# Weight sums behind the gates, transposes spread over other pairs, and maxima's rows read ahead of values and keys in an mLSTM cell with a feed-forward block

## The chip, the cores and the metric

The kernel runs on one core of a Trainium2 chip. The metric is the device time of one execution in microseconds, the median of several runs. Three runs of the kernel before took 471.5, 471.28 and 469.67 us: median 471.28.

The core has five engines with queues of their own, each of which works through its instructions in the order of the program: PE (TensorE, matmuls; "PEld" is its weight load), DVE (VectorE), ACT (ScalarE), POOL (GpSimd) and SP, which here only issues DMAs. An instruction waits, with all that is behind it in its queue, until the semaphores that it names have the values it asks for.

## The reference

An mLSTM cell over 4 batches, 8 heads, 768 steps and a head size of 40, and then a feed-forward block with a quick GELU on its output (3072 tokens, 320 to 2048 to 320). All is float32.

```python
for t in range(S):
    m_new = np.maximum(f_gate[:, :, t] + m, i_gate[:, :, t])
    f_stab = np.exp(f_gate[:, :, t] + m - m_new)
    i_stab = np.exp(i_gate[:, :, t] - m_new)
    m = m_new
    C = f_stab[:, :, None, None] * C + i_stab[:, :, None, None] * np.einsum('bhd,bhe->bhde', vt, kt)
    n = f_stab[:, :, None] * n + i_stab[:, :, None] * kt
    h_tilde = np.einsum('bhde,bhe->bhd', C, qt)
    nq = np.einsum('bhd,bhd->bh', n, qt)[:, :, None]
    denom = np.maximum(np.abs(nq), 1.0)
    o = 1.0 / (1.0 + np.exp(-o_gate[:, :, t]))
    y[:, :, t] = o * h_tilde / denom
...
h = x @ w_in
g = h * (1.0 / (1.0 + np.exp(-1.702 * h)))
return (g @ w_out).astype(np.float32)
```

## The kernel before

The 768 steps are worked on in six chunks `w` = 0 to 5 of 128 steps. Within a chunk the recurrence is written as attention with weights: scores of queries and keys, times a matrix of exponentials, times values, plus a part that comes from the carried state. The main loop takes one chunk's feed-forward block at a time, and lays the attention of the next chunk beside it. It has two phases.

**Up phase** of chunk `w` (here for `w` from 1): `token_sums` (L679 to L684), and then `up_fast(w, j)` for the pairs `j` = 0 to 7, each the product of the tokens with two blocks of 128 hidden units. A Strassen-like scheme is used, so each pair has seven products of 128x256 on PE (L722) and sums around them. In one pair, ACT copies the first product `p1` out of PSUM (L761), DVE forms two sums with the second bank `p56` (L762, L763), then two more with row 1 of the result (L774, L775). ACT applies the GELU to the pair before (L690, first half 1, then half 0), copies row 0 to SBUF (L739), and POOL adds the sums to it (L781). For the last two pairs DVE does that add instead (L783). In pairs 0 and 4 the products of the last 64 input rows of four pairs are made together (L701, 16 matmuls on two halves of 64 rows). PSUM banks: p1, p56 and the rows of most pairs share four banks of the pool `ps_m`; rows of pairs 2, 3, 6 and 7 are in `ps_a`. Which bank a tile gets is settled when the program is built, and with it which reader of an older tile PE must wait for.

Beside the up phase of `w` stands the preparation of `w + 1`:
- `gates(w + 1)` after pair 0, on DVE: two running scans (L288, L296), with L290 between them (two operands in SBUF), and small steps up to `both` (L325, L326). It issues on SP the DMAs of the maxima to DRAM (`m_row`, L304 and two of L307), of the stacked gates (`st_row`, L330) and of `both` (`d_row`, L331).
- `load` brings the o gate (`eo`, 640 KB), the values (`v_st`, 640 KB in 3 DMAs) and the keys (`k_st`, 640 KB in 3 DMAs), in pieces of 160 bytes.
- `columns_in` reads `st_row` and `d_row` back as columns (`raw`, four DMAs L350 and one L352); `spread` reads `m_row` back, copied to all partitions (`wt`, four DMAs of 256 KB, L403).
- `block_transposes(w + 1, n)` for n = 0 to 7 turns the keys (even n) and queries (odd n) of one batch on DVE (L394).
- In chunk 1 only, `weight_sums(j)` for j = 0 to 3, on POOL: sums of the output weights (L803), which the down phase needs.
- `hidden_difference` (L812) and `hidden_sums` (L820, L823) prepare the down phase, mostly on POOL.

**Down phase** of chunk `w`: 14 products `down_fast` (L844 on PE, added up by DVE in L849), and after some of them a step of the attention of `w + 1`: `columns` (L367, L371 on ACT), `scale` (values times weights, `vw`, L588 on POOL), `decay` (L579), `weights` (32 exponentials on ACT, L435, and a triangular mask on POOL, L439), `carry` (L602 on PE; needs `vw` and the keys), `scores` (L459 on PE, product on DVE, L462), `values` (p_o, L503, and p_i, L511, on PE). L511's bank is that of the second half of the scores, so it comes free with the second L462.

Chunk 0 has ordinary products (L626, L635, L790) in place of the fast ones. Chunk 5 has no next chunk.

The order on each engine is the order in which the code calls; nothing reorders it. POOL's queue in chunk 1's up phase is L781 of pair 0, L803, L781 of pair 1, L803, L781 of pair 2, L803, L812, L781 of pair 3, L803, and so on. SP's queue from the last stretch of one down phase on is: keys and queries of `w + 1` in squares (8 DMAs of 320 KB, L108), the o gate, the five DMAs of the gates, values, keys, `raw`, `wt`, the gate inputs of `w + 2` (L92). SP and ACT share eight semaphores for their DMAs: each DMA waits until the one that last used its semaphore, about eight before it, has landed.

`wait_for(x)` (L590) copies one column of `x` to a tile `mark` on POOL, so that POOL's queue stands until `x` is there. The kernel before uses it once, in chunk 0.

Of the kernel before, what the change touches and what calls it, by code (L numbers as in the profile page):

```python
# [8 lines left out]
FP = mybir.dt.float32  # L9
# [17 lines left out]
def kernel(  # L27
# [14 lines left out]
    BH = B * H  # L42
# [17 lines left out]
    gate = ctx.enter_context(tc.tile_pool(name="gate", bufs=2))  # L60
# [49 lines left out]
    def load(w, what, bs=slice(0, B)):  # L110
        hs = slice(bs.start * H, bs.stop * H)
        for c in what:
            if c == "o" and w not in eo:
                eo[w] = ld.tile([L, BH, D], FP, tag="eo", bufs=1, name="eo")
            dst, src = {"k": (k_of(w), k), "q": (q_st, q), "v": (v_st, v), "o": (eo.get(w), o_gate)}[c]
            if w and c in "kv":
                for i, t, r in ((0, slice(0, L), slice(0, L)), (1, slice(0, HL), slice(HL, L)),
                                (1, slice(HL, L), slice(0, HL))):
                    x = src[:, :, w * L + t.start:w * L + t.stop, :].rearrange("b (p two) s d -> two s (b p) d", two=2)
                    nc.sync.dma_start(out=dst[r, i::2, 0:D], in_=x[i])  # L120
                continue
            nc.sync.dma_start(out=dst[:, hs, 0:D],
                              in_=src[bs, :, w * L:(w + 1) * L, :].rearrange("b h s d -> s (b h) d"))
# [98 lines left out]
    state = [const.tile([128, BH // 2, D1], FP, name=f"state{i}") for i in range(2)]  # L222
    state_mid = const.tile([128, BH // 2, D1], FP, name="state_mid")

    m_at = {0: m0}
    cols, stacked, m_row, raw = {}, {}, {}, {}
    kT, qT, ys, xT, gs, o_ps, sums, vw, x_row = {}, {}, {}, {}, {}, {}, {}, {}, {}

# [53 lines left out]
    def gates(w):  # L282
        m = m_at[w]
        swapped = gate.tile([3 * BH, L], FP, bufs=1, name="f_run")
        f_run = swapped[0:BH, :]
        m_run = gate.tile([BH, L], FP, bufs=1, name="m_run")
        st = stacked[w] = gate.tile([3 * BH, L], FP, bufs=1, name="st")
        V.tensor_tensor_scan(out=f_run, data0=ones, data1=f_sb[w], initial=0.0, op0=OP.mult, op1=OP.add)  # L288
        a = st[0:BH, :]
        V.tensor_tensor(out=a, in0=i_sb[w], in1=f_run, op=OP.subtract)  # L290
        if w == 0:
            room = work.tile([L, H, D1], FP, tag="u", name="room").rearrange("p h d -> p (h d)")
            neg, part = room[0:BH, 0:L], room.bitcast(BF)[0:BH, 2 * L:3 * L]
            V.tensor_tensor(out=neg, in0=f_run, in1=i_sb[w], op=OP.subtract)
            split(G, a3, neg, neg, part)
        V.tensor_tensor_scan(out=m_run, data0=ones, data1=a, initial=m, op0=OP.mult, op1=OP.max)  # L296
        if w == 0:

            room = work.tile([L, H, D1], FP, tag="u", name="room").rearrange("p h d -> p (h d)")
            left, part = room[0:BH, 0:L], room.bitcast(BF)[0:BH, 2 * L:3 * L]  # L300
            split(V, m3, m_run, left, part)
        else:
            to = m_row[w] = rows.tile([2, BH, HL], FP, name="m_row")
            side_queue(w).dma_start(out=to[:, 0::2].rearrange("n h t -> h n t"),  # L304
                              in_=m_run[0::2].rearrange("h (n t) -> h n t", t=HL))
            for n in range(2):
                side_queue(w).dma_start(out=to[1 - n, 1::2], in_=m_run[1::2, n * HL:(n + 1) * HL])  # L307
        end = m_run[:, L - 1:L]
        if w + 1 < NW:
            m_at[w + 1] = gate.tile([BH, 1], FP, name="m_end")  # L310
            V.tensor_tensor(out=m_at[w + 1], in0=f_run[:, L - 1:L], in1=end, op=OP.add)

        mid = m_run[:, HL - 1:HL]
        for x, (old, new) in enumerate(((m, mid), (mid, end)) if w else ((m, end),)):
            t = slice(x * HL, x * HL + HL) if w else slice(0, L)
            V.tensor_scalar(out=st[BH:2 * BH, t], in0=m_run[:, t], scalar1=old, scalar2=None, op0=OP.subtract)
            V.tensor_scalar(out=st[2 * BH:3 * BH, t], in0=a[:, t], scalar1=new, scalar2=-1.0, op0=OP.subtract,
                            op1=OP.mult)
        if w:
            for x in range(2):  # L320
                V.tensor_scalar(out=swapped[:, x * HL:(x + 1) * HL], in0=st[:, (1 - x) * HL:(2 - x) * HL], scalar1=odd,
                                scalar2=None, op0=OP.mult)
            V.scalar_tensor_tensor(out=swapped, in0=st, scalar=even, in1=swapped, op0=OP.mult, op1=OP.add)
            both = gate.tile([BH, 2], FP, name="both")
            V.tensor_tensor(out=both[:, 0:1], in0=m, in1=mid, op=OP.subtract)  # L325
            V.tensor_tensor(out=both[:, 1:2], in0=mid, in1=end, op=OP.subtract)  # L326
            st_row = rows.tile([L // 32, 3 * BH, 32], FP, name="st_row")
            d_row = rows.tile([BH, 2], FP, name="d_row")
            stacked[w] = st_row, d_row
            side_queue(w).dma_start(out=st_row.rearrange("n k t -> k n t"), in_=swapped.rearrange("k (n t) -> k n t", t=32))  # L330
            side_queue(w).dma_start(out=d_row, in_=both)  # L331
# [257 lines left out]

    def wait_for(x):  # L590

        G.tensor_copy(out=mark, in_=x[:, 0:1])

    def carry(w, c):
        js = slice(c * NJ, (c + 1) * NJ)
# [333 lines left out]
    for w in range(NW):  # L929
        more = w + 1 < NW  # L930
        if w == 0:
            for j in range(NF // 2):
                if j % 2 == 0:
                    ahead, behind = converted[j // 2]
                    run([(convert, p) for p in ahead] + [(fetch, p) for p in fetched.get(j // 2, ())])
                    up(w, j, lambda: run([(columns_turn, 1) if p is None else (convert, p) for p in behind]))
                if j == 6:
                    load(1, "o")
                if j == 1:
                    wait_for(w_in_sb[:, 1, 512:1024])  # L940
                    scale(0, 1)
                    load(1, "v")
                if j < B and j % 2:
                    carry(0, j // 2)
                if j == 3:
                    masks()
                    gates(1)
                    columns_in(1)
                if j == 4:
                    spread(1)  # L950
                    load_squares(1, "q")
                if j >= B:
                    transposes(1, j - B)
        else:
            token_sums(w)
            if more:
                load(w + 1, "o")
            for j in range(NF // 2):
                up_fast(w, j)
                if more and j == 0:  # L960
                    gates(w + 1)
                if w == 1 and j < 4:
                    weight_sums(j)
                if more and j == 2:
                    load(w + 1, "vk")
                    columns_in(w + 1)
                    spread(w + 1)
                if more and j:
                    for n in ((0, 2), (4, 6), (1,), (3, 5), (7,), (), ())[j - 1]:
                        block_transposes(w + 1, n)  # L970
                if more and j == 7:
                    columns_turn(w + 1)
                if 2 <= j < 6:
                    hidden_difference(w, j - 2)
                if j >= 6:
                    hidden_sums(w, (j - 6,), G)
            gelu_fast(w, NF // 2 - 1)
            hidden_sums(w, (2, 3), V)
        side = attention(w + 1) if more else {}
        if w == 0:  # L980

            blocks = [(lambda b=b, n=n: down(w, b, n)) for n0 in (0, 2) for b in range(B) for n in (n0, n0 + 1)]
        else:
            blocks = down_fast(w, 0) + down_fast(w, 1)
        for i, block in enumerate(blocks):
            if w == 0 and i in (0, 4, 5):
                convert((17, 18, 19)[max(i - 3, 0)])
                if i == 0:
                    for n in (1, 3, 5, 7):
                        block_transposes(1, n)  # L990
            if w + 2 < NW and i == (6 if w == 0 else 0):
                load_gates(w + 2)
            if w + 2 < NW and i == 13:
                load_squares(w + 2, "kq" if w else "k")
            if w == 0 and i == 15:
                load_squares(w + 2, "q")
            block()
            run(side.get(i, []))
            if w == 0 and i in (11, 13):
                input_sums(slice(0, 4) if i == 11 else slice(4, 8))  # L1000
# [30 lines left out]
```

## Time and profile before

The profiled execution took 470.63 us, of which the span from the first to the last instruction is 468.9 us, at a TensorE clock of 1.00 throughout. It is 0.65 us below the median of the three runs.

| stretch | from, us | to, us | length | PE busy | DMA share |
|---|---|---|---|---|---|
| chunk 0's attention and start | 0 | 23 | 23.0 | 21.47 | 0.90 |
| chunk 0 up | 23 | 66.3 | 43.3 | 42.82 | 0.99 |
| chunk 0 down | 66.3 | 109.45 | 43.15 | 43.15 | 0.59 |
| chunk 1 up | 109.45 | 145.83 | 36.38 | 33.69 | 0.92 |
| chunk 1 down | 145.83 | 185.2 | 39.37 | 39.37 | 0.29 |
| chunk 2 up | 185.2 | 217.3 | 32.1 | 32.10 | 1.05 |
| chunk 2 down | 217.3 | 257.55 | 40.25 | 40.01 | 0.33 |
| chunk 3 up | 257.55 | 290.27 | 32.72 | 32.72 | 0.95 |
| chunk 3 down | 290.27 | 330.6 | 40.33 | 39.62 | 0.31 |
| chunk 4 up | 330.6 | 363.1 | 32.5 | 32.50 | 0.99 |
| chunk 4 down | 363.1 | 403 | 39.9 | 39.48 | 0.34 |
| chunk 5 up | 403 | 434.9 | 31.9 | 31.90 | 0.03 |
| chunk 5 down | 434.9 | 468.9 | 34.0 | 30.51 | 0.06 |

The stretches are cut by hand at the first matmul of a phase, to within 0.6 us. By the first matmuls themselves the up phases of chunks 2 to 5 last 32.64, 32.67, 32.50 and 31.9 us. PE busy is the time in which at least one matmul runs; a slow stretch in which matmuls overlap less counts as busy too. A DMA share over 1 means that packets overlap on the 16 DMA engines. Of the other engines DVE is the fullest in chunk 1's up phase, with 30.77 of 36.38 us, and POOL has 26.60 there against 14.57 in chunk 2's.

### The profile page before, as it was taken

To read this page: it belongs to the slowest core of one execution; us is meant where nothing else is said; L and a number is where in the kernel's file an instruction comes from. 1 tells how busy PE (TensorE), PEld (TensorE's weight loads), DVE (VectorE), ACT (ScalarE), POOL (GpSimd) and SP (SyncE) were. 2 spreads that over 40 slices of the span, in tenths; PEclk is the share of its full clock that TensorE was granted. 3 is DMA by queue.
4 is the path that set the end of the run, shared out by engine and by line. 5 is a ranking of instruction groups with operands and counts; after the bars stand their busy time and mean duration, and the time that the engine had idled before them with its cause. 6 is when DMAs were issued, how large, how long until landed. Compare 5 with 4: busy or idle time off the path is not lost.

```text
span 468.9 us, 12393 instructions
## 1 busy us (share of the span) xinstructions
PE 459.3 (98%) x5071; PEld 390.7 (83%) x5071; DVE 352.9 (75%) x738; ACT 185.8 (40%) x433; POOL 164.1 (35%) x153
## 2 busy tenths in 40 slices
PE   8999999999989999999999999999999999999997
PEld 6867877776759999769999769989888999787996
DVE  6788998798987876887875896877797866553712
ACT  5686778000546600545800345720254630064200
POOL 5101508001697600266700257610147630146200
PEclk9999999999999999999999999999999999999999
DMA  8999899049995035979324977305999405100000
GB/s 166 195 287 237 172 254 208 4 105 206 152 101 118 3 81 129 192 94 118 72 60 113 198 103 114 97 27 130 170 145 107 106 17 129 39 1 1 1 28 29
DMA packets 135561, 52.87 MB, mean 113 GB/s; under 512 B 101984, under 2 KB 131632, under 8 KB 135504
## 3 DMA queue, kind: packets, MB, share of 16 engines
q1 hardware_dynamic: 127136, 50.27, 55.7%
q10 hardware_dynamic: 8048, 1.66, 1.8%
q8 instruction: 40, 0.66, 0.6%
q0 software_dynamic: 320, 0.15, 0.1%
q14 instruction: 17, 0.14, 0.1%
HBM read 44.52 MB, written 7.54 MB: 111 GB/s over the span
## 4 chain that ended last, share of the span: by engine, by line
PE 78%; ACT 6%; POOL 5%; DMA 4%; DVE 3%; SPq 3%; issue 1%; POOLq 0%; DVEq 0%; ACTq 0%
PE p_out L844 25%; PE p_h L722 21%; PE p_h L701 8%; PE p_out L790 8%; PE p_h L626 6%; ACT wt L435 5%; DMA wt<-m_row 3%; PE p_i L511 2%; PE p_h L635 2%; PE p_o L503 2%; POOL wt L439 1%; PE p_c L602 1%; POOL s L823 1%; DMA s_in<-in_moe_w_in_dram 1%; POOL s L820 1%
## 5 line engine op out<-in xcount | busy, mean ns | idle before, releaser
L781 POOL TENSOR_TENSOR g<-g,parts 128x512 f32<-128x512 f32 x30 | 38.2, 1272 | 197.2 <-ACT g L739 184.7
L761 ACT COPY parts<-p_h 128x256 f32<-128x256 f32 x40 | 14.9, 372 | 156.0 <-PE p_h L722 150.8
L844 PE MATMUL p_out<-w_out_sb,g 128*128 128x160 f32 x480 | 68.9, 300 | 0.0
L844 PEld LDWEIGHTS p_out<-w_out_sb,g 128*128 128x128 f32 x480 | 66.4, 190 | 0.5
L722 PE MATMUL p_h<-xT,w_in_sb 128*128 128x256 f32 x240 | 66.0, 384 | 0.0
L690 ACT ACTIVATE g<-g 128x512 f32<-128x512 f32 x80 | 47.7, 629 | 27.2 <-DVE g L775 22.6
L722 PEld LDWEIGHTS p_h<-xT,w_in_sb 128*128 128x128 f32 x240 | 44.5, 190 | 12.2 <-issue 6.3
L849 DVE TENSOR_TENSOR o_sb<-o_sb,p_out 128x160 f32<-128x160 f32 x70 | 21.1, 317 | 37.9 <-PE p_out L844 37.3
L844 PE MATMUL p_out<-t_sb,s 128*128 128x160 f32 x320 | 47.1, 300 | 0.0
L844 PEld LDWEIGHTS p_out<-t_sb,s 128*128 128x128 f32 x320 | 44.4, 190 | 0.2
L722 PE MATMUL p_h<-t_x,s_in 128*128 128x256 f32 x160 | 41.3, 380 | 1.5 <-DVE parts L763 1.1
L435 ACT ACTIVATE wt<-wt,cols 128x64 f32<-128x64 f32 x160 | 38.8, 333 | 6.2 <-DMA wt<-m_row 6.2
L701 PE MATMUL p_h<-xT,w_in_x 64*128 64x512 f32 (+1 forms) x200 | 39.4, 517 | 0.0
L790 PE MATMUL p_out<-w_out_sb,g 128*128 128x320 f32 x128 | 35.7, 436 | 0.0
L722 PEld LDWEIGHTS p_h<-t_x,s_in 128*128 128x128 f32 x160 | 30.2, 190 | 6.4 <-DVE parts L763 1.5
L762 DVE TENSOR_TENSOR t_x<-p_h,parts 128x256 f32<-128x256 f32 x40 | 17.0, 426 | 24.2 <-ACT g L690 12.7
L701 PEld LDWEIGHTS p_h<-xT,w_in_x 64*128 64x128 f32 x200 | 19.6, 186 | 16.1 <-issue 14.2
L739 ACT COPY g<-p_h 128x512 f32<-128x512 f32 x30 | 17.4, 580 | 38.7 <-PE p_h L701 16.8
L790 PEld LDWEIGHTS p_out<-w_out_sb,g 128*128 128x128 f32 x128 | 23.9, 190 | 9.6
L626 PE MATMUL p_h<-xT,w_in_sb 128*128 128x256 f32 x128 | 29.6, 384 | 0.0
L775 DVE TENSOR_TENSOR g<-p_h,parts 128x512 f32<-128x512 f32 x40 | 27.7, 692 | 1.4
L439 POOL TENSOR_SCALAR_AFFINE_SELECT wt<-wt 64x1024 f32<-64x1024 f32 x20 | 23.6, 1178 | 13.2 <-ACT wt L435 12.5
(204 smaller groups left out, 859.9 us busy)
## 6 DMA issues: line engine op xcount, KB each, us to landing
q_sq<-in_q_dram SPq DMA_DIRECT2D x20, 320.0 KB, 10.9
wt<-m_row SPq DMA_DIRECT2D x20, 256.0 KB, 5.7
k_sq<-in_k_dram SPq DMA_DIRECT2D x16, 320.0 KB, 6.3
out_dram<-o_sb SPq DMA_DIRECT2D x24, 160.0 KB, 1.9
eo<-in_o_gate_dram SPq DMA_DIRECT2D x5, 640.0 KB, 10.7
bits<-in_moe_w_in_dram SPq DMA_DIRECT2D x6, 512.0 KB, 10.1
q_sq<-x_row SPq DMA_DIRECT2D x10, 256.0 KB, 3.0
v_st<-in_v_dram SPq DMA_DIRECT2D x14, 160.0 KB, 5.8
```

Of the source, the lines that this page charges most:

```text
L435: A.activation(out=x[:, h, :], in_=x[:, h, :], func=AF.Exp, scale=-1.0, bias=cols[w][:, c * PH + h:c * PH + h + 1])
L439: G.affine_select(out=r, in_=r, compare_op=OP.is_ge, fill=0.0, base=0, pattern=[[0, PH], [1, HL]], channel_multiplier=-1)
L626: T.matmul(ph[j][i][:, t], w_in_sb[:, c, f * 128:(f + 1) * 128], x[:, c, t], start=(first and c == 0 and n == 0), stop=(not first and c == ...
L690: A.activation(out=gs[w, j][:, i, :], in_=gs[w, j][:, i, :], func=AF.Gelu_apprx_sigmoid)
L701: T.matmul(row[:, t], w_in_x[r, j, :], xT[w][r, 2].rearrange("p b t -> p (b t)")[:, t], start=(start and h == 0), stop=(not start and h == ...
L722: T.matmul(out, a, x[n], start=start, stop=stop)
L739: A.copy(out=g[:, 0, :], in_=row0)
L775: V.tensor_tensor(out=g[:, 1, :], in0=row1, in1=y[:, half_w:3 * half_w], op=OP.add)
L781: G.tensor_tensor(out=g0, in0=g0, in1=u, op=OP.add)
L790: T.matmul(po, gs[w, f // 2][:, f % 2, b * L:(b + 1) * L], w_out_sb[:, f, :], start=(f == 0), stop=(f == NF - 1))
L844: T.matmul(po, a(f), b[:, f, :], start=(f == 0), stop=(f == NH - 1))
L849: V.tensor_tensor(out=dst, in0=x, in1=po, op=OP.add)
```

## The change

There are three edits, all in how the work of chunk `w + 1` is laid beside the up phase of `w`.

1. In chunk 1, after the gates, POOL waits for `both` before it begins the weight sums. Only the first of the four is directly behind the wait. `wait_for` is generalised to a tile of fewer than 128 partitions.
2. The load of the o gate is called after the gates instead of before pair 0; `columns_in` and `spread` are called before the loads of values and keys instead of after.
3. The transposes are called after pair 1 (two), pair 3 (one), pair 4 (three) and pair 5 (two), where they were called after pairs 1 (two), 2 (two), 3 (one), 4 (two) and 5 (one).

```diff
-    m_at = {0: m0}
+    m_at, ends = {0: m0}, {}
...
-            both = gate.tile([BH, 2], FP, name="both")
+            both = ends[w] = gate.tile([BH, 2], FP, name="both")
...
     def wait_for(x):
-        G.tensor_copy(out=mark, in_=x[:, 0:1])
+        G.tensor_copy(out=mark[0:x.shape[0]], in_=x[:, 0:1])
...
             token_sums(w)
-            if more:
-                load(w + 1, "o")
             for j in range(NF // 2):
                 up_fast(w, j)
                 if more and j == 0:
                     gates(w + 1)
+                    load(w + 1, "o")
+                    if w == 1:
+                        wait_for(ends[w + 1])
                 if w == 1 and j < 4:
                     weight_sums(j)
                 if more and j == 2:
-                    load(w + 1, "vk")
                     columns_in(w + 1)
                     spread(w + 1)
+                    load(w + 1, "vk")
                 if more and j:
-                    for n in ((0, 2), (4, 6), (1,), (3, 5), (7,), (), ())[j - 1]:
+                    for n in ((0, 2), (), (4,), (6, 1, 3), (5, 7), (), ())[j - 1]:
                         block_transposes(w + 1, n)
```

On SP's queue the order becomes: squares, the five DMAs of the gates, the o gate, `raw` (five), `wt` (four), values (three), keys (three). On POOL one copy of 32x1 is added, between L781 of pair 0 and the first L803. PE and ACT have the same instructions in the same order; the PSUM banks of some pairs change in the built program. In chunks 1 to 4 the last bank of the rows of pair 5 is one that L763 of pair 4 frees, where it was one that L739 of pair 4 frees, and the first product of pair 5 has the one that L739 frees.

## The prediction

> **What bounds the kernel.** I read first the share of busy time: TensorE (PE) is busy for 98% of the span. So only PE's stalls and slow stretches can be won, and the next views are the waits of PE, its chain of work, and then the timelines of whatever released it.
>
> ```profile
> PE 459.3 (98%) x5071; PEld 390.7 (83%) x5071; DVE 352.9 (75%) x738; ACT 185.8 (40%) x433; POOL 164.1 (35%) x153
> ...
> PE p_h L722 <- DVE parts L763: 2.2, 2, 1.1
> PE p_i L511 <- DVE wt L462: 1.4, 3, 0.7
> ...
> PE p_h L722 <- ACT parts L761: 0.5, 1, 0.5
> ...
> 204.59 4.20 PE p_h L701 x16
> ...
> 422.09 3.63 PE p_h L701 x16
> ```
>
> Waits are total us, times, longest. The two waits of L722 on L763 and the one on L761 all lie in chunk 1's up phase (at 121.8, 129.5 and 136.6 us): 2.7 us. The three waits of L511 lie in the down phases of chunks 2, 3 and 4: 1.4 us. The last two lines are pieces of the chain: the same 16 matmuls take 4.20 us in chunk 2 and 3.63 in chunk 5, which prepares no next chunk. Chunks 1, 3 and 4 show 4.28, 4.21 and 4.22.
>
> Who is late in chunk 1, from DVE's and POOL's timelines (start, us, instruction; the second line is the same instruction in chunk 2):
>
> ```profile
> 116.55 2.81 DVE L290 TENSOR_TENSOR st<-fi,f_run 32x128 f32<-32x128 f32 x1
> ...
> 191.87 0.28 DVE L290 TENSOR_TENSOR st<-fi,f_run 32x128 f32<-32x128 f32 x1
> ...
> 116.21 3.01 POOL L803 TENSOR_TENSOR t_sb<-w_out_sb 128x1280 f32<-128x1280 f32 x1
> 122.98 1.28 POOL L781 TENSOR_TENSOR g<-g,parts 128x512 f32<-128x512 f32 x1 [3.77 <-DVE parts L763]
> ...
> 133.72 0.63 ACT L690 ACTIVATE g<-g 128x512 f32<-128x512 f32 x1 [0.65 <-POOL g L781]
> 134.26 0.57 ACT L739 COPY g<-p_h 128x512 f32<-128x512 f32 x1
> ```
>
> L290 stretches from 0.28 to 2.81 us just while the first weight sum (L803) runs, so the whole DVE queue runs 2.53 us late. The last two lines are the far end: POOL's add lets the gelu go, and only then is row 0 of pair 4 copied out.
>
> Who is late in the down phase, chunk 3, on SP's queue and on ACT:
>
> ```profile
> 266.02 8.82 SPq L304 DMA_DIRECT2D m_row<-m_run  x1
> ...
> 277.34 6.88 SPq L120 DMA_DIRECT2D v_st<-in_v_dram  x3
> 284.28 4.63 SPq L120 DMA_DIRECT2D k_st<-in_k_dram  x3
> 288.95 2.08 SPq L350 DMA_DIRECT2D raw<-st_row  x4
> ...
> 292.57 2.39 SPq L403 DMA_DIRECT2D wt<-m_row  x4
> ...
> 298.37 7.75 ACT L435 ACTIVATE wt<-wt,cols 128x64 f32<-128x64 f32 x32 [2.44 <-DMA wt<-m_row]
> ```
>
> The maxima's rows (L403) are issued behind values and keys; ACT's exponentials sit 2.44 us waiting for them (1.83 and 1.92 in chunks 2 and 4). Their delay runs through POOL's mask (L439) and DVE's product (L462) to p_i, whose bank that product frees.
>
> **The Trainium skill.** "SBUF — State Buffer", section "Who interferes with whom": a DVE instruction with two SBUF inputs contends with a GpSimd instruction that reads SBUF, and whichever comes second blocks fully. L290 agrees: it ends at 119.36, 0.14 after L803. "Perfetto Trace Analysis", "DMA Instruction — HWDGE (DVE, Sync)": a DMA's profiled window is lock wait and descriptor generation, not data. L304's 8.82 us for 8 KB agrees: it is the time that the eo load before it (640 KB, pieces of 160 B) took to leave the generator. "TensorEngine Tiling (Array Packing)", "Key Properties": row tiles run in parallel. The two 64-row halves of L701 do (starts 10 ns apart); in the 4.20 us blocks the last pair does not, since its second bank comes 0.5 us after the first.
>
> **1. The POOL wait, chunk 1.** Removed: 2.53 us of DVE block (2.81 less 0.28). Added: one copy on POOL; the only L592 of the trace took 0.32 us. With the block gone, `both` is ready at 121.97-2.53 = 119.44. Behind the wait on POOL stand L803, then pair 1's add L781, and so on. L803 starts at about 119.65 and takes 2.9 (the later ones): L781 of pair 1 at 122.55 against 122.98. From there POOL has no slack: L781 (1.24 from start to start) and L803 (2.88) of pairs 1, 2 and 3, and an L812 (1.25) after each of the last two L803, stand back to back in the trace until pair 4's L781 has ended at 139. So POOL gains 0.43 us only, while DVE gains 2.5. PE's two waits on L763 (pairs 1 and 3) vanish: L763 of pair 1 ends at 120.3, wanted at 121.7; L763 of pair 3 at about 125.9, wanted at 127.7. What is late next is POOL: PE would reach pair 5 at 132.3, but in the changed program's list of waits pair 5's first product takes the bank of pair 4's row 0, which L739 frees. L739 follows the gelu, which follows POOL's add of pair 3: 0.43 earlier than before, so its end moves from 134.83 to 134.40 and pair 5 starts at 134.5, against 135.93. That is 1.4 us. The third wait (0.5) goes as well, because pair 5's second bank is no longer the one of its own first product. Sum for chunk 1: **1.9 us**. Bounds: if POOL did not hold the rest back, 2.7 plus the slow block 0.6 = 3.3. If L290 is slow for another cause than POOL, L803 starts at 122.2, pair 1's L781 at 125.1 and L739 ends 2.1 us later than now: pair 5 starts 1.1 us later, the third wait still goes, -0.6. I take 1.9, since L803's span fits L290's so closely.
>
> **2. Transposes, chunks 1 to 4.** Eight of 1.05 us stay eight; before pair 3 two fewer have run, before pair 4 two fewer, before pair 5 one fewer, before pair 6 as many. DVE's L775 of pair 3, and ACT's L739 that follows it, come 2.1 us earlier (204.5 to 202.5 in chunk 2). The three after pair 4 cost 3.15 us and lie beside the 3.63 us of L701: they end at about 209.1, when pair 5's second product ends. The two after pair 5 end at 213.2, before pair 6's at 213.9. If that cover failed, DVE has 1 to 1.7 us of waits at pairs 5 and 6 now. The last bank of L701's block now waits for L763 of pair 4 (204.4, wanted at 207), as in chunk 5, not for L739. So 4.20 becomes 3.63 in chunks 2, 3, 4: 3 x 0.57 = **1.7 us**; chunk 1's is in the sum above. Bounds 0.9 to 2.1 (with what chunks 2 to 4, at 32.6 us of up phase, show above chunk 5's 31.95).
>
> **3. The queues.** Moved past SP's queue: the eo load (1 DMA) behind the five of the gates; 5 raw and 4 wt DMAs ahead of 3 v and 3 k. m_row need no longer follow eo. The wt rows then land some 10 us earlier (about 217 instead of 227 in chunk 2), ACT's waits go, the mask of the second half is done about 1.8 to 2.4 us earlier, and p_i needs 0.2 to 0.7: **1.4 us** gone. Bounds 0 to 1.6. The price is on v and k. In chunk 2 the DMA engines finish q_sq at 199; then come, in the new order: the gates' rows (1 us), a near-empty stretch as the one now seen after d_row's 8-byte rows (203 to 210, share 0.38; I take 4 us of it), eo 4, raw 1.5, d_row 2, wt 5, v 4, k 4, all as long as now. That puts v at 220.5 and k at 224.5, against 215.0 and 218.8. POOL's L588 wants v at 221.5 and the carry (L602, now at 226.7) wants k at about 226. Covered, with 1 to 1.5 us to spare.
>
> Sum: 1.9 + 1.7 + 1.4 = 5.0 us. The profiled execution took 470.63 us (span 468.9 and 1.7 around it), so 465.6; it lies 0.65 below the median of the three runs, 471.28, which gives **466.2 us**.
>
> **Rivals.**
> - *Values and keys land too late* (slower). If the empty stretch lasts 7 us as now, or v and k take the 8 to 10 us that they take in chunks 3 and 4, k lands at 228 to 230 and the carry stands 2 to 4 us in each of chunks 2 to 4. From about 1.5 us of lateness it costs, from about 3 on average it eats all gain; at 4.5 us late: 466.2 + 3 x 3 = 475. For it: the DMAs of the queue land in the order of their issue in the trace, so what is put ahead delays what is behind. Against it: no transfer is added, and the last of them ends 2 us earlier than now in my sum.
> - *POOL takes all of chunk 1's gain*: 466.2 + 1.9 = 468.1. For it: POOL is packed from 122.98 to 139. Against it: the bank of pair 5 is a different one.
> - *The rows come no earlier*: in the program each DMA waits for the landing of the one eight before it, and wt's second half for eo's. Then part 3 is nothing and chunk 1 gives half: 471.28-1.7-0.9 = 468.7, or about no change if part 2 gives 0.9 only.
> - *All of chunk 1 comes free*: 471.28-3.3-1.7-1.6 = 464.7.
>
> **Numbers.** 0.5% (2.36 us) is about what a measurement can tell from no change; faster is below 468.9. Chances: forecast 0.58 (464.7 to 467.6), all of chunk 1 0.08, POOL 0.10, rows no earlier 0.09, late keys 0.15. Faster: 0.56 of the first, all of the second, 0.07 and 0.03 of the next two, 0.74. Same: 0.02, 0.03 and 0.05 of these, and 0.02 of mild late keys, 0.12. Slower: the other 0.13 of late keys and 0.01, 0.14. The range of 8 in 10 reaches from 463.7 to 470.2; late keys stay outside.
>
> **What would show it.** Right: L290 of chunk 1 near 0.28; L803 first at 119.6; no wait of PE on L763; a PE gap of about 2 us before pair 5 of chunk 1, released by L739; L701's second block at 3.63 in chunks 2 to 4; no wait of ACT on wt nor of p_i on L462. Wrong: L588 waiting for v, or L602 for k, at the start of a down phase; L290 still long; pair 6 waiting for transposes.

## The result, and the profile after

The changed kernel takes 466.18 us (median of five runs, 465.74 to 466.44), the kernel before, set beside it, 470.46 (five runs, 468.79 to 471.5, the three of the first section among them): a ratio of 0.991, 95% interval 0.9884 to 0.9935. The forecast was 466.2. The profiled execution took 465.77 us, its span is 464.1, 4.8 less than before.

The total hides how unevenly the parts came out. A phase is counted from its first matmul to the first of the next one, in PE's timeline; the table has the profiled executions, in us.

| | up 1 | down 1 | up 2, 3, 4 together | down 2, 3, 4 together |
|---|---|---|---|---|
| before | 36.38 | 39.42 | 97.81 | 119.92 |
| after | 35.80 | 39.40 | 95.55 | 118.03 |
| won | 0.58 | 0.02 | 2.26 | 1.89 |
| forecast | 1.9 | | 1.7 | 1.4 |

PE's waits of the changed kernel (total us, times, longest), then lines of chunk 1's up phase from the timelines of DVE, POOL, ACT and PE (start, us, instruction; in brackets the idle time ahead of it and what ended it):

```profile
PE p_h L722 <- ACT g L739: 2.0, 1, 2.0
PE p_idle L197 <- DVE one L203: 1.1, 1, 1.1
PE p_x L530 <- DVE y L478: 0.5, 1, 0.5
```

```profile
116.44 0.28 DVE L290 TENSOR_TENSOR st<-fi,f_run 32x128 f32<-32x128 f32 x1
...
119.40 0.17 POOL L592 COPY mark<-both 32x1 f32<-32x1 f32 x1 [3.27 <-DVE both L326]
119.54 2.90 POOL L803 TENSOR_TENSOR t_sb<-w_out_sb 128x1280 f32<-128x1280 f32 x1
122.41 1.27 POOL L781 TENSOR_TENSOR g<-g,parts 128x512 f32<-128x512 f32 x1
...
133.14 0.63 ACT L690 ACTIVATE g<-g 128x512 f32<-128x512 f32 x1 [3.42 <-POOL g L781]
133.67 0.57 ACT L739 COPY g<-p_h 128x512 f32<-128x512 f32 x1
...
134.29 0.98 PE L722 MATMUL p_h<-xT,w_in_sb 128*128 128x256 f32 x2 [2.04 <-ACT g L739]
```

This is the forecast chain step by step: L290 is short, the first L803 stands at 119.54 (119.65 was forecast), pair 1's add at 122.41 (122.55), and PE waits 2.04 us before pair 5 on L739, which stands behind a gelu that waits for POOL. Pair 5 starts at 134.29 (134.5). What the forecast lacked is the stretch behind that gap. Busy time by stretch of chunk 1's up phase (the columns are PE, PEld, DVE, ACT, POOL, the granted TensorE clock, DMA share and GB/s):

```profile
128.00:134.29 6.29, 4.26 (x19) 1.66 (x18) 4.86 (x8) 2.82 (x6) 6.29 (x4) 1.00 0.43 125
134.29:137.70 3.41, 3.41 (x9) 2.73 (x10) 0.51 (x2) 0.90 (x2) 3.41 (x3) 0.54 1.21 212
```

PE is "busy" for all of the second stretch, but at a clock of 0.54: its 128x256 matmuls follow each other every 0.427 us instead of every 0.216. Eight of them are stretched so, and these eight intervals add up to 1.66 us more than at full clock. The whole profile's mean clock (0.996) hides it.

In the other chunks: L701's second block in chunk 2, in PE's timeline of the changed kernel, where the kernel before has 4.27 us; ACT's exponentials without an idle time; and SP's queue with the new order.

```profile
203.58 3.70 PE L701 MATMUL p_h<-xT,w_in_x 64*128 64x512 f32 x16
```

```profile
221.43 7.75 ACT L435 ACTIVATE wt<-wt,cols 128x64 f32<-128x64 f32 x32
```

```profile
196.99 0.32 SPq L331 DMA_DIRECT2D d_row<-both  x1
199.37 0.40 SPq L122 DMA_DIRECT2D eo<-in_o_gate_dram  x1
203.40 2.45 SPq L350 DMA_DIRECT2D raw<-st_row  x4
205.95 0.37 SPq L352 DMA_DIRECT2D raw<-d_row  x1
206.44 2.58 SPq L403 DMA_DIRECT2D wt<-m_row  x4
209.07 5.28 SPq L120 DMA_DIRECT2D v_st<-in_v_dram  x3
```

The last wt row of chunk 2 lands at 214.19, seven us before ACT begins; v lands at 218.36 (220.5 was forecast) and L588 starts at 221.06, k at 222.28 (224.5) and the carry at 225.17. Not all chunks have so much to spare: in chunk 3 v lands at 291.94 and L588 starts at 292.29.

### The profile page after: what moved, and what is told of

Same layout as the page of the kernel before. It is cut to its first block, busy times and chain, and to the rows that moved or that the text cites. A ratio compares the mean times of both kernels' runs of the same rounds, so it can differ in the third digit from the quotient of the medians.

```text
span 464.1 us, 12384 instructions
## 1 busy us (share of the span) xinstructions
PE 456.6 (98%) x5071; PEld 391.2 (84%) x5071; DVE 349.2 (75%) x738; ACT 185.8 (40%) x433; POOL 162.8 (35%) x154
## 3 DMA queue, kind: packets, MB, share of 16 engines
q10 hardware_dynamic: 8048, 1.66, 1.8%
## 4 chain that ended last, share of the span: by engine, by line
PE 88%; SPq 4%; DMA 2%; issue 2%; DVE 2%; POOL 1%; ACT 1%; DVEq 0%; POOLq 0%; ACTq 0%
PE p_out L844 33%; PE p_h L722 24%; PE p_out L790 8%; PE p_h L701 7%; PE p_h L626 5%; SPq L122 3%; PE p_c L602 3%; PE p_o L503 2%; PE p_s L459 2%; PE p_i L511 2%; DMA s_in<-in_moe_w_in_dram 2%; PE p_h L635 2%; POOL g L781 1%; SPq L167 0%; PE p_t L386 0%
## 5 line engine op out<-in xcount | busy, mean ns | idle before, releaser
L781 POOL TENSOR_TENSOR g<-g,parts 128x512 f32<-128x512 f32 x30 | 38.2, 1272 | 196.5 <-ACT g L739 187.7
L722 PEld LDWEIGHTS p_h<-xT,w_in_sb 128*128 128x128 f32 x240 | 44.9, 191 | 14.2 <-issue 5.5
L435 ACT ACTIVATE wt<-wt,cols 128x64 f32<-128x64 f32 x160 | 38.8, 334 | 0.1
L701 PE MATMUL p_h<-xT,w_in_x 64*128 64x512 f32 (+1 forms) x200 | 37.1, 514 | 0.0
L701 PEld LDWEIGHTS p_h<-xT,w_in_x 64*128 64x128 f32 x200 | 18.5, 186 | 14.9 <-issue 13.9
L739 ACT COPY g<-p_h 128x512 f32<-128x512 f32 x30 | 17.5, 582 | 31.1 <-PE p_h L701 17.5
L626 PEld LDWEIGHTS p_h<-xT,w_in_sb 128*128 128x128 f32 x128 | 23.6, 190 | 5.3 <-issue 2.4
```

The costliest lines, as they stand in the source:

```text
L435: A.activation(out=x[:, h, :], in_=x[:, h, :], func=AF.Exp, scale=-1.0, bias=cols[w][:, c * PH + h:c * PH + h + 1])
L626: T.matmul(ph[j][i][:, t], w_in_sb[:, c, f * 128:(f + 1) * 128], x[:, c, t], start=(first and c == 0 and n == 0), stop=(not first and c == ...
L701: T.matmul(row[:, t], w_in_x[r, j, :], xT[w][r, 2].rearrange("p b t -> p (b t)")[:, t], start=(start and h == 0), stop=(not start and h == ...
L722: T.matmul(out, a, x[n], start=start, stop=stop)
L739: A.copy(out=g[:, 0, :], in_=row0)
L781: G.tensor_tensor(out=g0, in0=g0, in1=u, op=OP.add)
```

## The experiments

Theory A after reading this profile: chunk 1 is bound by POOL's packed queue, so the POOL wait only moved the stall from pairs 1 and 3 to pair 5, and a gap of that length is paid twice, since the clock is halved behind it. Rival B: the three parts are worth what the prediction's sum says, each by itself. The runs first split the change, then attack the gap.

**The POOL wait alone** (the kernel before, with part 1 only):

```diff
                 if more and j == 0:
                     gates(w + 1)
+                    if w == 1:
+                        wait_for(ends[w + 1])
```

> The kernel before with part 1 alone: POOL waits for chunk 2's gates ahead of the first weight sum; transposes and queues as before. Theory A (POOL's packed chain is the bound of chunk 1's up phase, and a PE gap of about 2 us costs its own length and then halved clock): L290 falls to 0.28 us and PE's waits on L763 vanish, but the matmuls of L701's last bank wait for ACT's L739 of pair 4, which ends near 134.4 us; the up phase of chunk 1 takes 35.5 to 36.5 us against 36.38, the run 470 to 471 us on the scale of a before of 470.5. Rival B (the sum of the prediction, the wait is worth most of 1.9 us by itself): up phase 34.5 to 35, run 468.6 to 469.

Measured: ratio to before 1.0038 (1.0023 to 1.0053), slower. Up 1 takes 37.31 us, 0.9 more than before, beyond what either theory expected. L290 is short and the waits on L763 shrink from 2.2 to 0.2 us, but the last pair of L701 waits for L739 of pair 4. PE's waits and its busy time by stretch:

```profile
PE p_h L701 <- ACT g L739: 1.6, 1, 1.6
...
PE p_h L722 <- ACT parts L761: 0.5, 1, 0.5
```

```profile
134.90:139.50 4.60, 4.08 (x9) 2.25 (x10) 0.01 (x1) 1.31 (x4) 4.60 (x4) 0.64 1.39 146
```

Behind that gap the clock falls again, and pair 5 runs through the third wait (0.46 us) and its first products at half speed. By itself the wait is a loss: it turns two gaps of 1.1 us at full clock into one of 1.6 with a slow stretch behind it. The mean clock of the single executions, which one slow stretch brings to 0.996, says the same: of the 22, three kept 1.000 and took 468.73 to 469.57 us, no more than the kernel before (median 469.75), and the 19 at 0.996 or less took 470.21 to 474.52.

**The change without the POOL wait** (parts 2 and 3):

```diff
                     load(w + 1, "o")
-                    if w == 1:
-                        wait_for(ends[w + 1])
```

> The changed kernel without part 1 (no POOL wait), parts 2 and 3 kept. Theory A: L290 takes 2.8 us again and PE waits 1 to 1.4 us on L763 of pair 1; PE then reaches pair 5 about 1.3 us later, so its gap there is 1.3 us or less, the clock stays at full speed, and pair 5 starts only 0.5 us later than in the changed kernel; the up phase of chunk 1 takes 34.6 to 34.9 us against 35.80 and the run 465.0 to 465.3 us, FASTER than the changed kernel by about 1 us. Rival B (the wait is worth its gain): 466.6 to 467.5 us.

Measured: 465.41 us, ratio 0.9903 (0.9879 to 0.9926); the changed kernel has 0.991 above and 0.9887 in its second set of runs below, so the two can't be told apart by the total. In the trace up 1 takes 34.61 us, 1.2 less than with the wait, as theory A has it:

```profile
PE p_h L722 <- DVE parts L763: 1.1, 1, 1.1
...
PE p_h L722 <- ACT g L739: 0.9, 1, 0.9
PE p_s L459 <- DVE state L611: 0.8, 1, 0.8
```

```profile
134.00:137.70 3.70, 2.88 (x13) 2.57 (x14) 2.58 (x5) 1.67 (x4) 3.70 (x3) 1.00 0.63 211
```

The gap is back at pair 1, the one before pair 5 is 0.9 us and the clock behind it stays at 1.00. But 0.84 us come back in the down phase (the third line of the waits). POOL's own work there is not late: L588 starts 4.7 us after the phase's first matmul, as in the changed kernel. Yet POOL stands idle for only 0.42 us before it, against 2.17, so POOL's last sums reach further into the phase, and DVE's sums lie beside POOL's work. DVE's timeline in the changed kernel (the phase starts at 145.15), then without the wait (143.99):

```profile
147.63 1.35 DVE L820 TENSOR_TENSOR s<-g 128x512 f32<-128x512 f32 x2
148.89 1.29 DVE L823 TENSOR_TENSOR s<-s,g 128x512 f32<-128x512 f32 x2
...
155.22 0.50 DVE L611 TENSOR_TENSOR state_mid<-p_c,state_mid 128x328 f32<-128x328 f32 x1 [0.85 <-PE p_c L602]
```

```profile
146.47 2.33 DVE L820 TENSOR_TENSOR s<-g 128x512 f32<-128x512 f32 x2
148.73 3.48 DVE L823 TENSOR_TENSOR s<-s,g 128x512 f32<-128x512 f32 x2
...
155.21 0.49 DVE L611 TENSOR_TENSOR state_mid<-p_c,state_mid 128x328 f32<-128x328 f32 x1
```

Three of the four sums take 1.67 to 1.78 us in place of 0.69, and L611, for which PE waits, comes no earlier although the phase starts 1.16 us earlier. As with L290, DVE's instructions, each with two operands in SBUF, stretch while POOL works. So much of what PE wins in chunk 1 comes out of POOL's lead over it. Theory A missed that return.

**The changed kernel again**, to see whether gap and clock belong to one execution:

> The changed kernel once more, on the same chip as the parts below. 466 to 466.5 us; a PE gap of about 2 us before pair 5 of chunk 1, released by L739, and a granted clock near 0.55 in the 3.4 us behind it. If that gap and clock were an accident of the one profiled run, they are absent here.

Measured: 466.4 us, ratio 0.9887 (0.9852 to 0.9923). The gap before pair 5 is 2.1 us, the clock 0.58 between 137 and 140 us, up 1 takes 35.86: neither was an accident of one execution. The slow stretch is not in all of them, though. By their mean clock (0.995 or 0.996) 9 of the 11 executions of both sets have it; the two at 1.000, in this set, took 465.19 and 465.53 us, the four others of the set 466.07 to 467.23. In this profile v lands at 222.55 in chunk 2, L588 starts 5.7 us after the phase's first matmul in place of 4.7, and that down phase takes 40.19 us instead of 39.39: the price of part 3, in one execution.

**The new spread of the transposes alone** (part 2):

```diff
-                    for n in ((0, 2), (4, 6), (1,), (3, 5), (7,), (), ())[j - 1]:
+                    for n in ((0, 2), (), (4,), (6, 1, 3), (5, 7), (), ())[j - 1]:
```

> The kernel before with part 2 alone (the new spread of the transposes). Theory A (the spread, not the POOL wait, brings chunk 1's gain too): chunk 1's up phase as without the wait, 34.6 us instead of 36.38, of which 0.8 comes back in the down phase; chunks 2 to 4 lose 0.8, 0.8 and 0.6 of their up phases; p_i's waits on L462 (1.4 us) stay. 467 us on the scale of a before of 470.3. Rival B (the parts as in the prediction, 1.7 us for this one): 468.4 to 468.8, with chunk 1 at 36.

Measured: ratio 0.9981 (0.9951 to 1.001), no difference that can be told. Theory A's total (467 of 470.3, 0.993) lies outside the interval. Rival B's (0.996 to 0.997) lies within it, but its chunk 1 of 36 us does not come. The up phases win all that theory A expected: 34.61 in chunk 1 and 95.55 in chunks 2 to 4. The down phases give most of it back: 122.48 us in chunks 2 to 4 against 119.92, and 40.20 in chunk 1, there by DVE's stretched sums as without the POOL wait. PE's waits, and ACT's timeline in chunk 3:

```profile
PE p_i L511 <- DVE wt L462: 1.7, 3, 0.7
PE p_out L844 <- DVE s L820: 1.5, 2, 0.9
...
PE p_s L459 <- DVE state L611: 1.0, 2, 0.7
```

```profile
298.15 2.02 ACT L435 ACTIVATE wt<-wt,cols 128x64 f32<-128x64 f32 x8 [2.76 <-DMA wt<-m_row]
```

The down phase of chunk 3 starts at 288.72, 1.55 us earlier than before, but the last wt row lands at 300.10 against 300.45: the queue of transfers does not move with PE. Everything that waits for its end (ACT's L435, and on DVE L356, behind which L820 stands) is about as late as before, and PE waits for it. Chunk 4 shows the same (373.11 against 372.81); in chunk 2 the last row came 0.80 us earlier with the phase, and only 0.05 us was given back. In chunks 3 and 4 the gain of the transposes is real only because part 3 takes those rows out of the way.

**The queues alone** (part 3, both moves), and **of these only the swap** of values and keys with the rows, with the o gate left ahead of the gates:

```diff
                 if more and j == 2:
-                    load(w + 1, "vk")
                     columns_in(w + 1)
                     spread(w + 1)
+                    load(w + 1, "vk")
```

> The kernel before with part 3 alone (eo behind the gates, raw and wt rows ahead of v and k). The down phases of chunks 2 to 4 lose 0.3, 0.9 and 0.6 us, chunk 1 and all up phases stay: 468.3 to 468.6 us. Rival (rows no earlier): no difference, 470.3.

> Of part 3 only the swap of v and k with the raw and wt rows; eo stays ahead of the gates. Theory A (the rows have about 6 us to spare in the new order, and eo ahead takes 4 of them): the same gain as with the whole of part 3, 468.3 to 468.6 us, and ACT's L435 does not wait. Rival (m_row behind eo is what made the rows late): L435 still waits for wt and half or more of the gain is missing, 469.3 or more.

Measured: 0.9942 (0.9925 to 0.996) with both moves. Its down phases take 118.07 us, 1.85 less, and all other phases stay, as expected. With the swap only 1.0013 (0.9991 to 1.0035): the gain is gone. Theory A misses; the rival has the total, but not the reason. L435 no longer waits for wt, but v and k are late. PE's waits and SP's queue in chunk 2:

```profile
PE p_c L602 <- POOL vw L588: 1.8, 2, 1.1
PE p_c L602 <- DMA k_st<-in_k_dram: 1.5, 1, 1.5
```

```profile
194.16 0.40 SPq L122 DMA_DIRECT2D eo<-in_o_gate_dram  x1
194.66 8.90 SPq L304 DMA_DIRECT2D m_row<-m_run  x1
...
209.46 2.63 SPq L403 DMA_DIRECT2D wt<-m_row  x4
212.15 7.79 SPq L120 DMA_DIRECT2D v_st<-in_v_dram  x3
```

This is the prediction's rival "values and keys land too late", in a kernel that differs by one moved line. With eo ahead, m_row sits 8.90 us in the queue, d_row lands at 208.98 (203.50 in the changed kernel), and v at 225.30, where L588 would start near 223.5 (4.7 us after the phase's first matmul, as in the changed kernel). Moving eo behind the gates lets the small rows through first, and it is this move that makes the swap pay.

**Attacking the gap.** If POOL's queue is what holds chunk 1, work taken off POOL must win the gap and the slow stretch together. Pairs 3 and 4 of chunk 1 get the path of the last two pairs, where DVE adds row 0 straight from PSUM:

```diff
-        apart = j < NF // 2 - 2
+        apart = j < NF // 2 - 2 and not (w == 1 and j in (3, 4))
```

> The changed kernel, but in chunk 1 the row-0 adds of pairs 3 and 4 go to DVE, straight from PSUM (as pairs 6 and 7 have it): two L781 and two L739 fewer, two L783 more. Theory A (POOL is the bound there): the gap before pair 5 and the half-clock stretch behind it vanish together; up phase of chunk 1 32 to 32.5 us instead of 35.80; if the sums on POOL follow 2.5 us earlier the whole 3.4 to 3.7 us stay won: 462.3 to 463 us. Rival C (another engine is as late, ACT or DVE): the gap moves to pair 6 or 7 and at most 1.5 us is won: 464.7 or more.

Measured: 461.99 us, ratio 0.9827 (0.9802 to 0.9853). Up 1 takes 31.99 us, near chunk 5's 31.84; nothing is given back. PE's busy time in the same two stretches:

```profile
128.00:134.29 6.29, 6.29 (x29) 3.55 (x28) 6.08 (x10) 2.75 (x7) 6.29 (x4) 1.00 0.48 125
134.29:137.70 3.41, 3.41 (x17) 3.00 (x16) 3.34 (x7) 1.21 (x3) 3.41 (x3) 1.00 1.18 209
```

17 matmuls run where the changed kernel had 9. This version beats both kernels. But besides POOL's adds the edit takes away the copy that PE waited for (L739 of pair 4), so by itself it can't tell POOL's load from the order on ACT. The next run can.

The other way to take the wait away leaves POOL's work as it is, and lets ACT copy row 0 before the gelu that waits for POOL:

```diff
+        if k != 2:
+            copy_row()
         if j:
             gelu_fast(w, j - 1)
...
         if apart:
-            if k != 2:
-                copy_row()
```

> The changed kernel, with ACT's copy of row 0 (L739) issued ahead of the gelu of the pair before, in all pairs. It takes the wait away where the gap shows (L739 of pair 4 no longer stands behind a gelu that waits for POOL), and leaves POOL's work as it is. Theory A: the gap before pair 5 goes, but POOL's add of pair 4 still ends at 138.4, the gelu of pair 4 holds ACT until then, and PE stalls before pair 7 instead, on ACT's copies of pair 6: 464.7 to 466.2 us, 0 to 1.5 us won. Rival D (only the place of the copy in ACT's order was the matter): all of 3.7 us won, 462.5 us.

Measured: 463.92 us, 0.9868 (0.9843 to 0.9894), between the two expectations, and not for the reason that theory A gave: up 1 falls to 32.00 us, with no stall before pair 7. What comes back is in down 1, 40.92 us: L588 now follows POOL's last sum with no idle time at all, at 148.66, 6.7 us after the phase's first matmul in place of 4.7. So PE's gap came from the copy's place behind a gelu that waits for POOL. POOL's load itself is paid for in the down phase: as without the POOL wait, its lateness is carried over the phase boundary, here to L588 too.

**The POOL wait again, with POOL relieved** (pairs 3 and 4 on DVE, without part 1):

> The kernel with the adds of pairs 3 and 4 on DVE, but without part 1 (no POOL wait). Theory A (the wait is worth its 1.1 to 1.4 us of PE stalls on L763 once POOL is no longer the next bound; in the changed kernel it only moved the stall): L290 2.8 us, PE waits about 1.1 us on L763 of pair 1, no gap before pair 5, clock at full speed; chunk 1's up phase 33.3 us instead of 31.99, the run 463.0 to 463.8 us against 462.0 with the wait. Rival (the wait is worth nothing in any case): 461.8 to 462.3.

Measured: 463.95 us, 0.9874 (0.9851 to 0.9896), just above theory A's range; up 1 takes 33.60 us against 31.99 with the wait, and PE waits 1.1 us on L763 once more. The wait is worth 1.6 us of that phase, and nothing measurable in the changed kernel.

**The o gate last** (pairs 3 and 4 on DVE; eo behind v and k):

```diff
                 if more and j == 0:
                     gates(w + 1)
-                    load(w + 1, "o")
...
                     load(w + 1, "vk")
+                    load(w + 1, "o")
```

> The kernel with the adds of pairs 3 and 4 on DVE, and eo's load (640 KB) put behind v and k instead of ahead of the raw and wt rows. Theory A (eo is what stands between the gates and v, some 3.5 us of transfer): v and k land 3 to 4 us earlier against L588 in chunks 2 to 4, L588 never waits for them, eo still lands before L374 wants it; the median stays within 0.5 us of 462.0, and the runs lie closer together than the 0.8 us of spread there. Rival (eo late in its turn, ACT's L374 waits for it, and what follows it): 463 or more.

Measured: 462.38 us (461.87 to 462.51), 0.984 (0.9821 to 0.9858): no gain over 461.99, as forecast; the spread of four runs, 0.6 us, shows no clear difference from 0.8. v lands 4.5 us ahead of L588 in chunk 2 instead of 2.1; k, 2.8 us ahead of the carry instead of 2.3, gains less than forecast. It buys room only: the changed kernel's second profile, above, is the one where that room was missing.

**The lock and the clock by themselves.** Without the POOL wait, the first weight sum was issued twice, and then one and a half times; the second issue writes the same numbers again.

> The changed kernel without the POOL wait and with the first weight sum issued twice in a row (the same numbers written again), which lengthens PE's wait at pair 1 of chunk 1, a place where full-tile matmuls (L722) run ahead of it. Theory A (POOL's sum locks DVE out, one instruction at a time, and a PE gap of 1.6 us or more halves the granted clock for the next 3 to 4 us wherever it lies): two DVE instructions stretch instead of one, pair 1's L763 is 2.5 to 2.9 us later still, PE's gap there is 3.5 to 4 us and the clock behind it near 0.5. Rival E (the halved clock belongs to the block of 64-row matmuls, L701, ahead of the gap before pair 5): the same gap, the clock stays at 1.00. Rival F (DVE is blocked once only): the gap stays near 1.1 us.

> The changed kernel without the POOL wait, and the first half of the first weight sum issued a second time right behind it (the same numbers written again): a second lock of DVE of half the length. It should make PE's gap at pair 1 of chunk 1, behind full-tile matmuls, 2.2 to 2.7 us long, about as long as the gap of 2.0 us before pair 5 that had the clock halved. Theory A (a gap of about 2 us is enough wherever it lies): granted clock near 0.55 for some 3 us behind it. Rival E ([...]the block of 64-row matmuls ahead of pair 5 counts as half idle): the clock stays at 1.00 behind a gap of 2.2 to 2.7 us.

Measured, one profile each. First the sum issued twice: DVE's timeline, and the busy time of the stretch behind PE's gap; then the same two of the run with one and a half:

```profile
117.21 2.81 DVE L290 TENSOR_TENSOR st<-fi,f_run 32x128 f32<-32x128 f32 x1
120.05 3.08 DVE L296 TENSOR_TENSOR_SCAN m_run<-one,m_end,st 32x128 f32<-32x128 f32 x1
```

```profile
126.10:129.90 3.80, 3.74 (x10) 3.00 (x11) 3.66 (x8) 1.52 (x3) 3.65 (x2) 0.55 0.39 28
```

```profile
116.39 2.81 DVE L290 TENSOR_TENSOR st<-fi,f_run 32x128 f32<-32x128 f32 x1
119.23 1.72 DVE L296 TENSOR_TENSOR_SCAN m_run<-one,m_end,st 32x128 f32<-32x128 f32 x1
```

```profile
124.90:128.20 3.30, 3.30 (x8) 2.52 (x8) 3.16 (x7) 1.52 (x3) 3.30 (x3) 0.50 0.42 21
```

In these two runs each sum on POOL holds one DVE instruction until the sum has ended: L296, 0.47 us in the changed kernel, stretches to 3.08 with a whole second sum and to 1.72 with half of one. So L290's length is POOL's doing. PE's gaps are 3.7 and 2.3 us, behind full-tile matmuls, and the clock halves behind both; at these lengths the block of 64-row matmuls (rival E) is not needed for it.

## Why the prediction was right

The total came within 0.1 us, from three terms of which one was too large and two too small: 0.58 for 1.9, 2.26 for 1.7, 1.89 for 1.4, and 0.1 more from the start of the program. The errors cancelled, and that is luck. So is a part of the last step: the sum of 5.0 us was taken off a median of 471.28 us (which gives 466.28, written as 466.2). Beside the changed kernel the kernel before has a median of 470.46, so the medians differ by 4.28 us, the profiled executions by 4.86.

1. *The POOL wait, chunk 1.* Each step held: the lock, the freed DVE, POOL as the next bound (by way of the order on ACT), the bank of pair 5, the gap of about 2 us and its releaser. The mis-sized term is the worth of that earlier start: "pair 5 starts at 134.5, against 135.93. That is 1.4 us", plus the third wait. Pair 5 did start then, and in the profiled execution 1.66 us were lost behind it to the halved clock. The prediction foresaw a gap of 2 us and priced it at its own length. Its "sum for chunk 1" was also laid at the door of the wait; the runs show that the spread of the transposes brings it (34.6 us with parts 2 and 3 or part 2 alone, 37.31 with the wait alone), and that the wait lengthens the up phase until POOL is relieved or the copy moved.
2. *The transposes.* The 0.57 us per block was right (4.27 to 3.70 in the same view). The rest, 0.23 us each in chunks 2 and 3, is a delay of 0.13 us and a slow start of 0.10 behind it at pair 4 in the kernel before (chunk 2), too short to be listed as waits; they went with pair 3's earlier DVE chain. The stated bounds reached 2.1, so 2.26 lies just outside.
3. *The queues.* The waits of p_i were counted as the 1.4 us that the profile lists. The phases won 1.89. The products of p_o and p_i around the first of each chunk's waits lost 0.33, 0.79 and 0.63 us, 0.08 to 0.21 more than the wait that is listed (0.24, 0.71 and 0.42), in matmuls that start late without PE ever being idle; in chunk 3 another 0.17 us lay in the scores.
4. *The rivals.* Late values and keys did not happen in the profiled execution: v and k landed 2 us earlier than estimated in chunk 2, if not in every execution. The run with the swap alone shows that the mechanism and the price were real. "The rows come no earlier" fell with L435's lost wait. "POOL takes all of chunk 1's gain" came near in size (0.58 of 1.9 was left), but pair 5 did start when it was forecast to, and the halved clock took the rest.
5. *What the sum can't show* is that parts 2 and 3 lean on each other. Part 2 alone gives 0.19% (from a loss of 0.1 to a gain of 0.49), part 3 alone 0.58%, both without the wait 0.97%. With these intervals the totals alone don't rule out that the two simply add up. The phases of the profiled executions do show it: in chunks 2 to 4 part 2 alone wins 2.26 us in the up phases and loses 2.56 in the down phases, and with part 3 nothing of it is lost.

## What to carry to other kernels

Before counting a stall as won, ask what the freed engine runs into next, and whether the transfers that feed the next phase move with it: a shorter phase in front of a queue of fixed length only waits at its end. Here one gap of 1.6 us or more cost more than several short ones of the same sum, so a change that gathers short gaps into one can lose time while it removes waits. When one engine's queue is packed, look first for work on it that a neighbour already knows how to do: two adds moved to DVE brought nearly as much as the whole change.

## What the runs showed of the hardware that was not expected

The granted clock fell to half behind PE gaps of 1.6 us (in the run with the wait alone), 2.0 and 2.1 (the changed kernel, twice), 2.3 and 3.7, for 3.41 us each time. In the profiled executions it stayed at 1.00 behind gaps of 0.9, 1.07 and 1.14, and behind one of 1.46 (the swap only, before the carry of chunk 4). The Trainium skill, "TensorE: Matmul & The Clock Gate", "Part 1: The HAM clock gate (the "warmup" mystery)", describes a gate that gives half the clock after an idle window of about 3.4 us and the whole again after about 3.4 us of work. The halving and the length of the slow stretch agree with the traces. The idle time doesn't: here less than half of that window was enough, and the measurement decides.

The slow stretch does not begin where the gap ends. In the changed kernel's second profile the gap lies between 132.84 and 134.92 us, and the first matmuls behind it still follow each other every 0.216 us; the clock falls at 136.11:

```profile
132.69:136.10 3.41, 1.32 (x7) 1.06 (x6) 2.03 (x3) 1.55 (x4) 3.41 (x2) 1.00 0.29 112
136.11:139.52 3.41, 3.41 (x10) 2.69 (x9) 1.87 (x4) 0.89 (x2) 3.41 (x4) 0.50 1.10 235
```

In the clock records of the five traces with a slow stretch, the full clock before it lasted, from its first rise, 129.71 us (three times) or 119.47 (twice), which is 38 and 35 times 3.413 us. So in these traces the clock changes only at marks 3.413 us apart, and the gap, or 3.3 us of the one of 3.7, lay between the two marks ahead of the slow stretch. That where a gap falls between the marks decides, and so why a few executions of one kernel have no slow stretch, would fit this, but no run here shows it.

The limit stays open. Idle time between two marks is not all that counts, or its limit is not fixed: 1.59 us halved the clock in the run with the wait alone, where 64-row matmuls stand on both sides of the gap, and 1.77 us at the end of the changed kernel's second profile did not. The kernel before, too, had a mean clock of 0.996 or less in 1 of 27 executions of one set and in 10 of the 46 fastest of another, and no trace shows where.
